# Attention, rational MLP and gated mixture on one core: the sign of 64-bit weights by parametric relu, early loads on ScalarE's queue, and extra matmuls behind attention's pieces

## The chip, the cores and the metric

The kernel runs on one core of a Trainium2 chip. The metric is the device time of one execution in microseconds; the engines are TensorE (PE, with its weight loads as PEld), VectorE (DVE), ScalarE (ACT), GpSimd (POOL) and SyncE (SP).

## The reference, cut to what is computed

Local attention over 4 batches of 8 heads, 576 positions of 64 values; four heads see the last 32 positions, four see every fourth of the last 128. Its output, as 2304 rows of 512, goes through a rational layer and then through eight experts with a gate that is balanced over rows and columns.

```python
x = attn_out.transpose(0, 2, 1, 3).reshape(B * S, H * D)
h = x @ w_in                                     # 512 -> 2048
P = a[0] + a[1]*h + a[2]*h**2 + a[3]*h**3
Q = 1.0 + abs(b[0])*abs(h) + abs(b[1])*h**2
x = (P / (Q + 1e-06)) @ w_out                    # 2048 -> 512
gate = balanced(exp(x @ w_gate - max))           # 8 rounds over rows and columns
out = sum(gate[:, e:e+1] * (relu(x @ w1[e]) @ w2[e]) for e in range(8))
```

`w_in` and `w_out` arrive as 64-bit floats; the kernel turns them into 32-bit floats itself.

## The kernel before

**Stages.** Batch 0 of attention runs first, by itself. Then 96 steps of the rational layer follow (`NS1`; six blocks of 384 rows, sixteen column blocks of 128), into whose slots, four to a step, the pieces of batches 1 (steps 0 to 7), 2 and 3, the conversion of weights and other side work are laid by hand with `at(slot, function)`. Then come the experts in 7-matmul units.

**Attention's pieces.** A batch is four pairs of heads with three groups of queries each. `att_pieces` gives 16 pieces `prep` (transposes of q or k into a PSUM bank, L347, evacuated by ACT, L355), 12 `qk` (mask matmul L363, scores L370; then DVE's maximum L388, ACT's exponentials L390, DVE's L394 and reciprocal L395, POOL's scaling L396), 12 `tr` (transposes of the weights, L405, evacuated at L410) and 12 `av` (L429; then a split into two 16-bit halves, ACT L229 and DVE L232). What a piece does after its matmuls is held back until the next piece has been laid down. In batch 0 the functions in `extra[i]` follow piece i (before: w_in's two first chunks asked for after pieces 12 and 30, w_gate's preparation after 20).

**The order of the work.** Each engine works off its own queue in order. The order on each queue is worked out by the framework from the order of the program, dependencies and priorities with estimated durations, so it is not always that of the text: conversions laid in later slots can stand earlier. `load` starts a transfer on SyncE's queue and makes it wait for the matmul last noted in `gate_mm`; in batch 0 that is the mask matmul of the last `qk` piece, later the first matmul of a step. Loads of v for attention (L302 to L315) wait on the same queue for their buffers.

**Conversion.** `to_f32` takes the high word of a 64-bit float as a 32-bit one, and ACT scales it by 2^-112 (L492); DVE shifts it left by 3, which drops the sign (L496), puts in three bits of the low word (L497), and the sign bit of the high word (L498). It runs on 16 pieces of w_in (four chunks `c` of four `kk`; `wi_conv`) and 16 rows of w_out (`wo_split`). ACT then takes each w_in piece's absolute maximum (L527), `wi_scale` makes a scale of it through a matmul (`across_max`, L180), and `wi_split` makes 16-bit halves, which the rational layer's matmuls (L631 to L633) read; its second layer is L691 to L693. The activation table is set once, at L239.

## Time and profile before

| | |
|---|---|
| median of 3 runs | 1973.75 us (1969.55 to 1974.08) |
| the profiled execution | 1978.19 us, its span 1976.1 us |
| PE busy | 1886.4 us, 95% of the span |
| DVE busy | 1567.5 us, 79% |
| ACT busy | 1217.0 us, 62% |
| POOL busy | 491.1 us, 25% |

Busy time is a sum of instructions' durations on an engine, without its waits; a matmul's end is modelled. The granted clock (PEclk) is 1.00 at 2.4 GHz and 0.50 at 1.2 GHz, and a value in between is a mean over a stretch. A row of the timeline gives the start, the duration, the instruction and, in brackets, how long its engine was idle before it and what ended that. `SPq` rows are the issue of transfers on SyncE's queue.

### The profile page before, as it was taken

What the parts mean: (1) busy time and instruction counts of PE and PEld (TensorE: products, weight loads), DVE (VectorE), ACT (ScalarE), POOL (GpSimd) and SP (SyncE); (2) the same over time, 40 slices, a digit from 0 to 9 for tenths busy, and PEclk for the clock granted to TensorE, in tenths of its full rate; (3) what the DMA queues carried; (4) which work ended last, traced back from release to release, by engine and by line L of the source; (5) the groups of instructions that cost most, each with busy time, mean ns of one, the idle gap of its engine ahead of it and who ended that gap; (6) DMA issues with size and microseconds to landing.
All of it is one profiled execution on the core that took longest, in us unless ns stands there. A gap on an engine that the chain in (4) does not pass through costs nothing. (4 is left out here: it accounts for less than half of the span.)

```text
span 1976.1 us, 36600 instructions
## 1 busy us (share of the span) xinstructions
PE 1886.4 (95%) x14202; PEld 1418.3 (72%) x14202; DVE 1567.5 (79%) x2564; ACT 1217.0 (62%) x2182; POOL 491.1 (25%) x489
## 2 busy tenths in 40 slices
PE   6688999998999999999999999999999999999998
PEld 5466777776767677767777777777777777777776
DVE  5797788799997998778787777877877787786754
ACT  5777777775776645646565664655555565555542
POOL 1232334321222113014212311411421141141111
PEclk7789999999999999999999999999999999999999
DMA  6643221124310451565356346345435625543323
GB/s 181 165 140 87 50 68 34 34 67 144 109 44 17 150 163 59 175 171 155 68 136 154 69 110 174 68 103 142 111 62 131 166 65 117 159 91 79 83 56 53
DMA packets 213133, 207.92 MB, mean 105 GB/s; under 512 B 78432, under 2 KB 160864, under 8 KB 212960
## 3 DMA queue, kind: packets, MB, share of 16 engines
q1 hardware_dynamic: 196096, 173.09, 29.1%
q0 software_dynamic: 16864, 32.51, 11.0%
q8 instruction: 111, 1.82, 0.4%
q14 instruction: 62, 0.51, 0.1%
HBM read 155.86 MB, written 49.68 MB: 104 GB/s over the span
## 5 line engine op out<-in xcount | busy, mean ns | idle before, releaser
L921 PEld LDWEIGHTS <-roomA 128*128 128x128 f16 x3276 | 319.7, 98 | 181.5 <-issue 14.6
L921 PE MATMUL l1a<-roomA 128*128 128x384 f16 x1872 | 357.0, 326 | 5.3 <-ACT roomV L970 4.2
L921 PE MATMUL l1b<-roomA 128*128 128x384 f16 x1404 | 273.6, 326 | 4.0 <-DVE roomA L972 1.9
L943 POOL TENSOR_TENSOR roomIG<-roomA 128x384 f32<-128x384 f32 x48 | 59.7, 1244 | 455.6 <-ACT roomA L977 354.6
L1021 PE MATMUL yps<-roomA 128*128 128x256 f16 x630 | 169.7, 273 | 2.2 <-DVE roomV L1047 1.5
L1022 PE MATMUL yps<-roomA 128*128 128x256 f16 x630 | 170.7, 273 | 0.8 <-DVE roomA L884 0.8
L1022 PE MATMUL yps<-roomA,roomV 128*128 128x256 f16 x630 | 170.5, 273 | 0.1
L677 POOL TENSOR_TENSOR roomIG<-roomA,roomIG 128x384 fp32r<-128x384 f32 x96 | 116.6, 1225 | 213.6 <-ACT roomIG L676 184.1
L1023 PE MATMUL yps<-roomA,roomV 128*128 128x256 f16 x630 | 169.6, 273 | 0.0
L1023 PE MATMUL yps<-roomA 128*128 128x256 f16 x630 | 168.9, 273 | 0.0
L1021 PE MATMUL yps<-roomA,roomV 128*128 128x256 f16 x630 | 168.8, 273 | 0.1
L692 PE MATMUL o1ps<-roomIG,roomV 128*128 128x384 f32 x384 | 136.2, 355 | 4.0 <-POOL roomIG L677 3.8
L870 POOL TENSOR_TENSOR roomA<-roomA 128x256 f32<-128x256 f32 x140 | 130.7, 953 | 35.2 <-DVE roomA L884 23.3
L631 PE MATMUL h1ps<-roomA 128*128 128x384 f16 x384 | 130.5, 340 | 8.8 <-ACT p L390 4.2
L884 DVE SCALAR_TENSOR_TENSOR roomA<-roomA,sm 128x768 f16<-128x768 f32 (+1 forms) x92 | 114.5, 1257 | 24.7 <-ACT roomA L881 23.9
L693 PE MATMUL o1ps<-roomIG,roomV 128*128 128x384 f32 x384 | 130.6, 340 | 0.0
L632 PE MATMUL h1ps<-roomA 128*128 128x384 f16 x384 | 130.1, 339 | 0.3 <-DVE roomA L232 0.3
L633 PE MATMUL h1ps<-roomA 128*128 128x384 f16 x384 | 129.8, 338 | 0.0
L943 POOL TENSOR_TENSOR roomIG<-roomV 128x384 f32<-128x384 f32 x48 | 50.1, 1044 | 299.5 <-ACT roomV L977 248.7
L691 PE MATMUL o1ps<-roomIG,roomV 128*128 128x384 f32 x384 | 107.5, 363 | 15.9 <-ACT roomIG L676 15.8
L1021 PEld LDWEIGHTS <-roomA 128*128 128x128 f16 x1008 | 98.7, 98 | 28.5 <-DVE roomA L1047 3.4
L881 ACT ACTIVATE roomA<-roomA,sm 128x768 f16<-128x768 f32 (+1 forms) x92 | 93.7, 1035 | 37.4 <-POOL roomA L870 17.8
(224 smaller groups left out, 4958.3 us busy)
## 6 DMA issues: line engine op xcount, KB each, us to landing
roomA<-xd SPq DMA_DIRECT2D x119, 384.0 KB
roomA<-in_moe_w_dram SPq DMA_DIRECT2D x256, 128.0 KB
roomA<-in_moe_w_dram SPq DMA_DIRECT2D x128, 256.0 KB
out_dram<-roomV POOLq DMA_DIRECT2D x31, 512.0 KB, 5.8
out_dram<-roomA POOLq DMA_DIRECT2D x31, 512.0 KB, 5.8
roomV<-in_moe_w_in_dram SPq DMA_DIRECT2D x16, 512.0 KB
roomA<-in_moe_w_out_dram SPq DMA_DIRECT2D x16, 512.0 KB
xd<-roomA SPq DMA_DIRECT2D x14, 384.0 KB
```

The lines of the kernel that those rows point to most:

```text
L631: mm = nc.tensor.matmul(hp, whi, xb[:, 0, kk, :], start=kk == 0, stop=False)
L632: nc.tensor.matmul(hp, whi, xb[:, 1, kk, :], start=False, stop=False)
L633: nc.tensor.matmul(hp, wlo, xb[:, 0, kk, :], start=False, stop=kk == KD - 1)
L677: nc.gpsimd.tensor_tensor(out=gl, in0=g, in1=gh.bitcast(F32), op=ALU.subtract)
L692: nc.tensor.matmul(ob[dd], hi, d["gl"], start=False, stop=False)
L693: nc.tensor.matmul(ob[dd], lo, d["gh"], start=False, stop=last)
L870: pin("p" if pool else "v", eng.tensor_tensor(out=d[:, o, :], in0=a, in1=b, op=ALU.add if w == 0 and n == 0 else ALU.subtract))
L884: pin("v", nc.vector.scalar_tensor_tensor(out=l, in0=x, scalar=sc, in1=h, op0=ALU.mult, op1=ALU.subtract))
L921: mm = nc.tensor.matmul(ps, w[:, wx_, wh, kk * P:(kk + 1) * P], x[:, xh, kk, :], start=start and kk == 0 and wh == 0 and xh == 0, stop=sto ...
L1021: nc.tensor.matmul(o, hh[:, a - 1, c], w[:, m, 0, :], start=i == 0 and half == 0, stop=False)
L1022: nc.tensor.matmul(o, hh[:, a - 1, c], w[:, m, 1, :], start=False, stop=False)
L1023: nc.tensor.matmul(o, hl[:, a - 1, c], w[:, m, 0, :], start=False, stop=i == NP - 1 and (last or half == 1 or b == 3))
```

## The change

The new `keep_busy` lays matmuls of 224 columns of the identity, read as 16-bit floats, behind the matmuls of a piece of batch 0 (four of them) or 1 (two), into columns of the same PSUM bank that the piece doesn't use; `prep`, `qk` and `av` pieces call it. In `to_f32` ACT applies a parametric relu with the slope -2^32 for negative values in place of a copy: a negative value becomes positive with an exponent higher by 32, whose bit DVE's shift moves to the sign. DVE's third operation goes. The first three loads of v for the maximum and those of w_in's chunks 0 and 1 move to ACT's queue, after pieces 4, 12 and 22; a `prep` piece of batch 0 now also notes its last matmul in `gate_mm`. Chunk 0 is converted after pieces 27 to 33 and split after 45 to 48, chunk 1 is converted after 37 to 46 and split in slots 2 to 8. w_gate is loaded at step 20 and prepared at step 26.

```diff
--- before.py
+++ after.py
@@ -20,7 +20,6 @@
 NEG = -1.0e9
 EXP_MASK = 0x7F800000
 ABS_MASK = 0x7FFFFFFF
-SIGN = -(1 << 31)
 TINY = 2.0**-80
 LN_SHIFT = 63
 
@@ -162,8 +161,8 @@
 
     gate_mm = [None]
 
-    def load(out, in_):
-        i = nc.sync.dma_start(out=out, in_=in_)
+    def load(out, in_, eng=nc.sync):
+        i = eng.dma_start(out=out, in_=in_)
         if gate_mm[0] is not None:
             tc.add_manual_dep(i.ins, gate_mm[0].name, mybir.DependencyInfo(mybir.DependencyClass.Sync, mybir.DependencyReason.DATA), reason="paced load")
 
@@ -240,6 +239,13 @@
     ident = cpool.tile([P, P], F32, name="ident")
     make_identity(nc, ident)
     nc.vector.memset(one, 1.0)
+    ident_w = ident.bitcast(BF16)
+
+    def keep_busy(bt, b, c, count):
+        if b < 2:
+            for _ in range(count):
+                nc.tensor.matmul(bt[:, c:c + 224], ident_w[:, 0:P], ident_w[:, 0:224], start=True, stop=True)
+
     ident_b = cpool.tile([D, P], BF16, name="ident_b")
     nc.vector.tensor_copy(ident_b.rearrange("p (h c) -> p h c", h=2), ident[0:D, 0:D].unsqueeze(1).to_broadcast([D, 2, D]))
     SEAMS = (0, None, None, None, 32, None, 0, None, 16, 48, -16, None)
@@ -344,7 +350,10 @@
         w, n = (QB, 3) if pr < 2 else (72, 4)
         bt = bank("qkps")
         for c in range(n):
-            nc.tensor.transpose(bt[:, c * w:(c + 1) * w], src[:, n * y + c, :], ident[:w, :w])
+            mm = nc.tensor.transpose(bt[:, c * w:(c + 1) * w], src[:, n * y + c, :], ident[:w, :w])
+        keep_busy(bt, b, HS, 4 - 2 * b)
+        if b == 0:
+            gate_mm[0] = mm.ins
 
         def after():
             if pr < 2:
@@ -374,6 +383,7 @@
                     start=False,
                     stop=i == 2,
                 )
+        keep_busy(bt, b, 3 * KW, 4 - 2 * b)
         sc = bt[:, 0:3 * KW].rearrange("q (i c) -> q i c", i=3)
         i = b * NG + pr * 3 + jj
         sx = sb.tile([P, 4, 3], F32, tag="asx", bufs=4, name="sx")
@@ -433,6 +443,8 @@
                     start=True,
                     stop=True,
                 )
+
+        keep_busy(bt, b, 288, 4 - 2 * b)
 
         def after():
             pos, end = GQ * jj, GQ * (jj + 1)
@@ -475,7 +487,7 @@
 
     def v_load(hf, i, tag):
         t = vst[hf, i] = stage_home(tag, "vst")
-        load(out=t, in_=vflat[hf, :, i * NV:(i + 1) * NV])
+        load(out=t, in_=vflat[hf, :, i * NV:(i + 1) * NV], eng=nc.sync if hf else nc.scalar)
 
     def v_scan(hf, i):
         t = vst.pop((hf, i))
@@ -489,13 +501,12 @@
     def to_f32(src, y, dst):
         w = src.rearrange("p (n two) -> p n two", two=2)
         lo, hi = w[:, :, 0], w[:, :, 1]
-        nc.scalar.activation(y, hi.bitcast(F32), AF.Copy, scale=float(2.0**-112))
+        nc.scalar.activation(y, hi.bitcast(F32), AF.Prelu, scale=float(2.0**-112), alpha=-float(2.0**32))
         d = y.bitcast(I32)
 
         def bits():
             nc.vector.tensor_scalar(out=d, in0=d, scalar1=3, scalar2=None, op0=ALU.logical_shift_left)
-            nc.vector.scalar_tensor_tensor(out=d, in0=lo, scalar=29, in1=d, op0=ALU.logical_shift_right, op1=ALU.bitwise_or)
-            nc.vector.scalar_tensor_tensor(out=dst.bitcast(I32), in0=hi, scalar=SIGN, in1=d, op0=ALU.bitwise_and, op1=ALU.bitwise_or)
+            nc.vector.scalar_tensor_tensor(out=dst.bitcast(I32), in0=lo, scalar=29, in1=d, op0=ALU.logical_shift_right, op1=ALU.bitwise_or)
 
         return bits
 
@@ -515,7 +526,7 @@
                 if kk % 2 == 0:
                     t = room(WI_ST[c][kk // 2], [P, 2, 1024], I32)
                 wst[c, kk] = t[:, kk % 2, :]
-                load(out=wst[c, kk], in_=src)
+                load(out=wst[c, kk], in_=src, eng=nc.scalar if c < 2 else nc.sync)
             else:
                 nc.sync.dma_start(out=wx[c][:, kk, :], in_=src)
 
@@ -570,7 +581,7 @@
     wi = [None] * 4
 
     def wi_scale(c):
-        return pow2_scale(wmx[:, 4 * c:4 * c + 4], 4, 14, s_wi[:, c:c + 1], i_wi[:, c:c + 1], lag=3 if c > 1 else 0, then=lambda: coefs(0, c, c + 1))
+        return pow2_scale(wmx[:, 4 * c:4 * c + 4], 4, 14, s_wi[:, c:c + 1], i_wi[:, c:c + 1], lag=3, then=lambda: coefs(0, c, c + 1))
 
     def wi_split(c, kk):
         if kk == 0:
@@ -584,8 +595,7 @@
     def wg_prep():
         m = cols()
         nc.vector.tensor_reduce(out=m, in_=wgr.rearrange("p k e -> p (k e)"), axis=AX, op=ALU.max, apply_absolute_value=True)
-        pow2_scale(m, 1, 4, s_wg, i_wg)
-        split16(wgr, wg[:, :, 0:NE], wg[:, :, NE:], s_wg)()
+        return pow2_scale(m, 1, 4, s_wg, i_wg, lag=3, then=lambda: split16(wgr, wg[:, :, 0:NE], wg[:, :, NE:], s_wg)())
 
     wo_hi, wo_lo = [], []
 
@@ -1136,7 +1146,7 @@
     LAG = 5
     ATT = ((1, 0, 7), (2, 7, 23), (3, 40, 62))
     WO = [f + f // 7 if f < 8 else 20 + 2 * (f - 8) for f in range(NF1)]
-    WI_S = (None, 0, 8, 14)
+    WI_S = (None, None, 8, 14)
 
     def att_pieces(b):
         groups = [(pr, jj) for pr in range(H // 2) for jj in range(3)]
@@ -1284,14 +1294,18 @@
             if callable(more):
                 at(s + 1, more)
 
-    for c in range(1, 4):
+    for kk in range(KD):
+        at(2 + 2 * kk, wi_split, 1, kk)
+    for c in range(2, 4):
         s = 4 * WI_S[c]
         for kk in range(KD):
             at(s + 1 + 2 * kk, wi_conv, c, kk)
-            at(s + (14 if c > 1 else 11) + kk, wi_split, c, kk)
+            at(s + 14 + kk, wi_split, c, kk)
         at(s + 10, wi_scale, c)
     for c in (2, 3):
         at(4 * WI_S[c] - (16 if c == 2 else 14), wi_load, c)
+    at(4 * 20, lambda: load(wgr, w_gate.rearrange("(k p) e -> p k e", p=P)))
+    at(4 * 26 + 1, wg_prep)
     for i in range(3):
         at(4 * 1 + 8 * i, v_load, 1, i, "x2_4")
         at(4 * (1 + 2) + 8 * i, v_scan, 1, i)
@@ -1305,27 +1319,26 @@
     att_load(0, 1, "R1")
     nc.sync.dma_start(out=abt[:, 0:4], in_=ra.partition_broadcast(P))
     nc.sync.dma_start(out=abt[:, 4:6], in_=rb.partition_broadcast(P))
-    for i in range(3):
-        v_load(0, i, f"x2_{3 + i}")
     att_load(0, 2, "R2")
     for i in range(2, 4):
         att_load_v(i)
     for i in range(4, 8):
         att_load_v(i)
-    nc.sync.dma_start(out=wgr, in_=w_gate.rearrange("(k p) e -> p k e", p=P))
     att_load(0, 3, "R3")
     pcs = att_pieces(0)
     extra = defaultdict(list)
+    extra[4].append(lambda: [v_load(0, i, f"x2_{3 + i}") for i in range(3)])
     extra[12].append(lambda: wi_load(0))
-    extra[30].append(lambda: wi_load(1))
+    extra[22].append(lambda: wi_load(1))
     av0 = next(i for i, pc in enumerate(pcs) if pc[0] == "av")
     extra[av0 - 1] += [lambda i=i: v_scan(0, i) for i in range(3)] + [lambda: v_scale(0), coef0]
-    extra[20] += [wg_prep]
     n = len(pcs)
     for kk in range(KD):
-        extra[30 + 2 * kk].append(lambda kk=kk: wi_conv(0, kk))
-        extra[n - 4 + kk].append(lambda kk=kk: wi_split(0, kk))
-    extra[n - 4 - 1].append(lambda: wi_scale(0))
+        extra[27 + 2 * kk].append(lambda kk=kk: wi_conv(0, kk))
+        extra[45 + kk].append(lambda kk=kk: wi_split(0, kk))
+        extra[37 + 3 * kk].append(lambda kk=kk: wi_conv(1, kk))
+    extra[40].append(lambda: wi_scale(0))
+    extra[50].append(lambda: wi_scale(1))
     for f in range(2):
         extra[44 + f].append(lambda f=f: wo_load(f))
     later = []
```

## Rows read from the trace of the kernel before

**Rows 1.** Busy time by stretch: us, then each engine's us (count), clock, DMA share.
```profile
0.00:68.90 68.90, 45.71 (x398) 35.52 (x398) 37.51 (x121) 38.92 (x146) 11.43 (x33) 0.69 0.73 196
...
4.40:20.00 15.60, 11.97 (x117) 9.69 (x117) 6.95 (x21) 6.78 (x30) 2.00 (x3) 0.89 0.77 232
20.00:36.00 16.00, 12.95 (x100) 9.82 (x99) 7.89 (x33) 7.67 (x33) 2.81 (x5) 0.60 0.57 121
36.00:52.80 16.80, 12.47 (x113) 9.57 (x111) 10.11 (x25) 11.83 (x45) 2.91 (x4) 0.57 0.60 177
...
58.70:68.90 10.20, 8.33 (x71) 6.41 (x71) 10.16 (x36) 10.20 (x36) 1.21 (x3) 0.50 1.13 269
...
68.90:150.00 81.10, 67.47 (x529) 48.74 (x529) 69.72 (x148) 62.17 (x189) 26.85 (x29) 0.84 0.43 130
150.00:200.00 50.00, 41.83 (x314) 29.62 (x313) 38.44 (x92) 37.41 (x103) 10.99 (x12) 0.93 0.32 86
200.00:320.00 120.00, 117.05 (x815) 88.19 (x812) 101.30 (x173) 93.52 (x208) 45.37 (x42) 0.99 0.22 58
...
470.00:500.00 30.00, 21.19 (x107) 16.93 (x106) 29.97 (x52) 14.49 (x24) 5.60 (x5) 0.83 0.26 77
...
1000.00:1800.00 800.00, 793.03 (x6063) 592.80 (x6062) 633.36 (x932) 463.18 (x667) 206.09 (x201) 1.00 0.47 113
```

**Rows 2.** Timeline, 68 to 72 us: start, us, instruction; first L631, later matmuls.
```profile
68.93 0.50 PE L631 MATMUL h1ps<-roomA 128*128 128x384 f16 x1
...
71.31 0.33 PE L632 MATMUL h1ps<-roomA 128*128 128x384 f16 x1
...
71.47 0.33 PE L633 MATMUL h1ps<-roomA 128*128 128x384 f16 x1
```

**Rows 3.** Waits until 68.9 us: who waited for whom, us, times, longest.
```profile
PE qkps L347 <- DMA roomA<-in_q_dram: 5.1, 2, 4.4
...
DVE sm L586 <- DMA wgr<-in_moe_w_gate_dram: 3.6, 1, 3.6
```

**Rows 4.** Timeline, 45 to 59 us: start, us, instruction, idle before it.
```profile
45.46 7.31 SPq L315 DMA_DIRECT2D roomA<-in_v_dram  x13
...
52.82 1.87 SPq L166 DMA_DIRECT2D roomV<-in_moe_w_in_dram  x4
...
57.17 0.66 ACT L492 ACTIVATE roomV<-roomV 128x512 f32<-128x512 f32 x1 [5.95 <-DMA roomV<-in_moe_w_in_dram]
...
58.76 0.85 PE L405 MATMUL ptps<-ident,roomA 128*96 128x128 f32 x3 [6.08 <-DVE roomA L232]
```

**Rows 5.** Timeline, 31 to 41 us.
```profile
31.48 0.79 PE L180 MATMUL mxps<-ident,sm 128*128 128x128 f32 x2 [1.02 <-DVE sm L586]
...
38.72 0.66 ACT L492 ACTIVATE roomV<-roomV 128x512 f32<-128x512 f32 x1 [4.30 <-DMA roomV<-in_moe_w_in_dram]
...
40.77 1.17 PE L429 MATMUL avps<-roomA 96*64 96x64 f32 x12 [2.09 <-ACT roomA L410]
```

**Rows 6.** Busy time in three finer stretches of batch 0.
```profile
24.00:30.00 6.00, 6.00 (x50) 4.42 (x49) 1.12 (x5) 3.03 (x12) 0.63 (x1) 0.50 0.38 85
46.00:50.00 4.00, 4.00 (x42) 3.41 (x44) 3.53 (x9) 3.56 (x14) 0.00 (x0) 0.50 0.49 109
50.00:52.70 2.70, 2.68 (x33) 2.00 (x30) 0.56 (x4) 1.22 (x8) 1.33 (x2) 0.91 0.22 49
```

**Rows 7.** Lines 498, 527, 166: min/median/max ns (L527: busy us, mean ns).
```profile
L498 DVE SCALAR_TENSOR_TENSOR roomA<-roomA x16: 660/684/1481, 74.3 to 316.6; 128x512 int32<-128x512 int32 x16
...
L527 ACT ACTIVATE roomV<-roomV 128x512 f32<-128x512 f32 x8 | 5.1, 634 | 0.0
...
L166 SPq DMA_DIRECT2D roomV<-in_moe_w_in_dram x16: 423/430/653, 33.3 to 177.2; - x16
```

**Rows 8.** Waits of PE, 68.9 to 200 us.
```profile
PE qkps L347 <- DVE roomA L657: 2.9, 2, 1.5
```

**Rows 9.** ACT's only table load: busy us, mean ns, idle before.
```profile
L239 ACT ACT_TABLE_LOAD x1 | 1.3, 1283 | 0.8 <-PEq L1405 0.8
```

## Prediction

> **What bounds the kernel now.** I read the table of stages first [rows 1]. From 1000 to 1800 us TensorE (PE) is busy 793 of 800 us and runs at its full clock, and between 200 and 320 us already 117 of 120; the one large hole in between is 470 to 500 us (21.2 of 30 us busy), where VectorE (DVE) is at 29.97 of 30. What comes after 200 us is therefore a stream of matmuls of fixed length, and a microsecond saved before it is a microsecond off the end, unless a new hole opens. The loss sits in front: until 68.9 us, where the first matmul of the rational layer (L631) starts [rows 2], PE is busy 45.7 us, and from there to 200 us 109 of 131 us, with clocks of 0.69, 0.84 and 0.93.
>
> The second view is who waited for whom before 68.9 us [rows 3]: PE 5.1 us for q, DVE 3.6 us for w_gate; and ScalarE (ACT) over 10 us for chunks of w_in, which the next view places. The timeline shows the largest of these [rows 4]: SyncE's queue spends 45.5 to 52.8 us on thirteen small loads of v, and only then issues the second chunk of w_in; ACT, first in, first out, stands at that chunk's conversion until 57.17 us, and PE starts nothing until 58.76 us, after 6.1 idle. The same pattern is smaller at 33 to 39 us and, for w_gate, at 28 to 32 us [rows 5].
>
> The third view is the granted clock in fine windows [rows 6]: 0.50 all through 24 to 30 us although PE counts as busy; up in the 51st us after four dense microseconds; and after the idle stretch of 52.7 to 58.7 us it is down to 0.50 for all of 58.7 to 68.9 us [rows 1].
>
> **The change part by part.** The sum is made on the profiled execution, 1978.2 us with a span of 1976.1, which lies 4.4 us over the median of 1973.75 us; differences are then taken off the median.
>
> *Batch 0, loads.* (a) The second chunk of w_in is asked for after piece 22 instead of 30, on ACT's queue, where no load of v stands before it. Landing took 4.35 us from issue [rows 4], so it is there some 20 us before its conversion. The hole of 52.8 to 58.7 us goes: -5.9. (b) The first chunk likewise after piece 12. ACT stood idle 4.3 us for it, PE 2.1 us after that [rows 5]: -2.1 to -4.3, taken as -3. (c) w_gate's preparation leaves batch 0 for step 26. DVE idled 3.6 us for it, PE 1.0 us [rows 3, 5]: -1.0 to -3.6, taken as -2.5, as the reciprocal of the softmax stood behind it on DVE. At step 26 its handful of operations of 0.1 to 0.3 us finds its data long landed: 0 to +1, taken as +0.5. What DVE waits for the coefficients stays: that load keeps its place on SyncE's queue.
>
> (d) The price is ACT's time. Eleven loads (three of v, eight of w_in) move to ACT's queue; SyncE took 0.43 us to issue one [rows 7], so 4.7 us of ACT, plus what each waits for the matmul that paces it; the exponentials and evacuations of attention are queued behind, and PE's next transposes wait for these. ACT is busy 38.9 of 68.9 us: 0 to +4.7, taken as +2. All transfers but the 16 KB of w_gate are the same bytes. At 46 to 52.7 us the DMA engines were busy 22 to 49% [rows 6] while the second chunk was missing, so what was late was the issue, behind SyncE's loads of v, and (a) and (b) count in full. The Trainium skill speaks against this part (DMA: Bandwidth & Descriptors, Issuing engines are not separate DMA queues): DMAs of all issuing engines run on the same 16 DMA engines, and several issuers save only issue time. By that alone (a) and (b) would give nothing, and the sum would be 9 us poorer; with a queue that waits for buffers, as here, the trace does not agree.
>
> *Sign by parametric relu.* (e) The third DVE operation of each conversion (L498) goes, 32 times 0.68 us [rows 7], 21.9 us of DVE in all, eight of them (5.4 us) in batch 0. There DVE was full (10.16 of 10.2 us) only from 58.7 us on [rows 1], where half of the eight stand: 0 to -5.4, taken as -2. ACT's operation is assumed as long as the copy it replaces, 0.66 us [rows 5]; the trace has no parametric relu, so I bound it by ACT's other operation over the same 512 columns, the absolute maximum (L527), 0.63 us [rows 7], and by it again with half as much on top: -0.03 to +0.3 us each, up to 10 us of ACT over 300 us in which it is busy some three quarters [rows 1]; taken as nothing.
>
> *Extra matmuls.* (f) Batch 0 has 40 pieces of the three kinds, so 160 extra matmuls of 224 bf16 columns, batch 1 has 80. A 384-column matmul starts every 0.16 us at full clock [rows 2], which is 0.32 at half, so an extra costs 0.095 or 0.187 us: 15.2 or 29.9 us in batch 0, 7.6 or 15 us in batch 1. They stand behind their piece on PE, and in the piece's own bank, so I let the evacuation wait for them: 0.38 or 0.75 us a piece in batch 0. What they can buy: by the clocks of [rows 1], 32 of the 45.7 us of PE before 68.9 us ran at half (80% of 20 to 36 us, 86% of 36 to 52.8, all of 58.7 to 68.9, 22% of 4.4 to 20). All at full clock, PE's work is 29.7 us, with the extras 44.9: as much as before. The gain is that nothing else slows down with it; I take 0, with bounds of -8 (half of the 16 us saved lies on the chain and the extras fill holes) and +20 (below).
>
> Batch 0 so far: -5.9 -3 -2.5 +2 -2 +0 = -11.4. L631 would start near 57.5 us.
>
> *Batch 1 and after.* (g) Twenty-four more L498 go, 16.4 us of DVE between 69 and 317 us. PE waited there for DVE's L657 2.9 us between 68.9 and 200 us [rows 8] and was idle 3.0 us between 200 and 320 [rows 1]: 0 to -6, taken as -4. (h) Clock: by the means of [rows 1] 26 us of 68.9 to 150 us and 7 us of the next 50 ran at half, worth some 14 us. These follow holes in which PE waits for ACT or DVE, and an extra stands behind the piece that waits, so it fills no hole; it only makes the rest denser. A quarter: -3 (0 to -8). (i) The 80 extras of batch 1 stand in a stage where PE is busy 83%: 0 to +15, taken as +4, about half of 7.6 us. (j) w_in's second chunk is split in steps 0 to 2 rather than 2 to 3: ACT and DVE work of the same size, 0.
>
> Batch 1 and after with w_gate: -4 -3 +4 +0.5 = -2.5. Together **-14**, so 1973.75 - 14 = **1960 us**.
>
> **The rivals.** *A, PE becomes the bound in batch 0 (slower).* If the extras don't bring the clock up, PE's 45.7 us stay, the extras cost 70% of 0.187 and 30% of 0.095 us, 25.5 us in all, and PE alone needs 4.4 + 71.2 = 75.6 us, 6.7 past 68.9, whatever the loads gain; batch 1 adds 5 or so of its 7.6 to 15 us. That gives 1985 us. It decides from a mean clock in batch 0 of about 0.7 downward. For it: 24 to 30 us, busy throughout and still at 0.50. Against it: the rise after 46 to 50 us, where PE ran without pauses, and that the idle stretch that sent the clock down at 57 us is gone.
>
> *B, the gain is hidden (no change).* ACT, with 4.7 us more to do and stopped by each load that waits for its pacing matmul, takes the place of the stalls, and the big chunks, now sent while the DMA engines carry v and the third pair's q and k at 77% [rows 1], make PE wait longer for small loads (5.1 us for q already, 4.4 of them in one wait [rows 3]). Terms (a) to (c) halve to -5.7, (d) goes to +4.7, the rest stays without the clock: -5.7 +4.7 -2 -4 +4 +0.5 = -2.5, 1971 us.
>
> *C, the change does not do what it says.* The trace has one table load on ACT, 1.28 us at the start [rows 9]. Were parametric relu in another table than the exponential, most of 32 conversions would be put between two more loads, up to 82 us of ACT; with half on the path, 2015 us. Against it: the copy, abs, exp and ln that share ACT now never cause a second load. The Trainium skill (ScalarE: Activation LUTs, Table sets: the hidden batching unit) says that cheap functions are in every set but does not name this one, and prices a switch at about 2.66 us, by which 64 switches would be an estimated 170 us; no row here has a second switch.
>
> **How the numbers follow.** Forecast 0.70, A 0.14, B 0.13, C 0.03. The forecast's own ends: with every unknown at its good bound some -35 us, at its bad bounds short of A about -3. 1940 to 1978 leaves out most of A, all of C, and the outermost tenth of the forecast. About 0.3%, 6 us, is what a measurement of this kernel tells from no change. The forecast is faster by more than that in nine of ten of its cases (0.63), B in a quarter of its own (0.03): 0.66. Within it lie the forecast's last tenth and most of B: 0.17. Slower: A and C, 0.17.
>
> **What would show it.** Right: L631 starts at 55 to 60 us; no wait of ACT for w_in before it; the clock of 20 to 50 us over 0.8; L498 of the old form gone with ACT's conversion at 0.66 to 0.68 us; still a single table load; from 320 us on the same picture, shifted. Wrong: a clock of 0.5 with PE busy without holes in batch 0 (A); ACT waiting for PE at the loads it now issues, or PE for q and k (B); table loads between conversions (C); or a hole of other length at 470 to 500 us, where DVE sets the pace and nothing is changed, which would move the end by several us for a reason not in the sum.

## The result, and the profile after

The changed kernel takes **1986.85 us** (median of 7 runs, 1982.56 to 1995.22) where the kernel before takes 1974.08: ratio 1.007 [1.0056, 1.0084]. It is slower by some 12.8 us; the forecast was 1960. Two stray executions of the experiments (7981 us of e5, 6214 us of the kernel before beside e9) are in a slow state and left out of the medians below. In the profiled execution (span 1983.3 us) the first matmul of the rational layer starts at 74.0 us, before at 68.9 [rows 2]; the forecast said 57.5.

The stages of the changed kernel, columns as in [rows 1] (stretch, then each engine's busy us, clock, DMA share):

```profile
0.00:68.90 68.90, 48.33 (x489) 37.86 (x489) 31.75 (x100) 38.12 (x139) 10.55 (x31) 0.88 0.73 196
68.90:150.00 81.10, 74.46 (x605) 51.56 (x606) 51.28 (x125) 56.56 (x178) 22.01 (x27) 0.87 0.40 123
150.00:200.00 50.00, 44.84 (x368) 33.72 (x366) 40.37 (x101) 43.01 (x117) 11.94 (x15) 0.97 0.34 96
200.00:320.00 120.00, 115.80 (x820) 88.03 (x819) 99.74 (x176) 95.62 (x212) 45.54 (x42) 1.00 0.22 58
470.00:500.00 30.00, 26.33 (x141) 20.74 (x140) 30.00 (x40) 16.14 (x26) 8.12 (x6) 0.94 0.42 122
1000.00:1800.00 800.00, 793.80 (x6064) 592.84 (x6063) 635.05 (x937) 463.68 (x669) 206.79 (x201) 1.00 0.48 115
...
500.00:520.00 20.00, 16.39 (x95) 11.49 (x94) 19.71 (x44) 12.59 (x21) 6.38 (x4) 0.91 0.27 91
```

The clock of the first 68.9 us rose from 0.69 to 0.88, as the extra matmuls were meant to do (without them, in e2 below, it is 0.66 again). The experts' row is the same. The hole of 470 to 500 us is spread out: PE is idle 3.7 us there and 3.6 us in the next 20, together 7.3 us from 470 to 520 where the kernel before has 9.0, with DVE at 30.00 of 30 and 19.71 of 20. From the start of step 64 to that of step 72, the steps around it, both kernels take the same time (43.1 us before, 42.9 after).

What took the place of the old stalls in batch 0 is in ScalarE's timeline (start, us, instruction, in brackets the idle time before it and what ended it; ACTq is ACT issuing a load):

```profile
22.36 2.01 ACTq L165 DMA_DIRECT2D roomV<-in_moe_w_in_dram  x4
24.41 0.49 ACT L420 ACTIVATE roomA<-ptps 96x384 f32<-96x384 f32 x1 [7.48 <-DMA roomA<-in_v_dram]
...
33.46 8.67 ACTq L165 DMA_DIRECT2D roomV<-in_moe_w_in_dram  x4
42.18 0.34 ACT L400 ACTIVATE p<-scps,sx 128x96 f32<-128x96 f32 x1 [9.54 <-DMA roomV<-in_moe_w_in_dram]
```

ACT stands 7.5 and 9.5 us **at its own loads of w_in**, with evacuations and exponentials queued behind. The loads of both queues tell of their landing by eight semaphores, taken in turn over SyncE and ACT together, and a load waits until the one eight earlier has landed. In the trace ACT stands from 16.9 to 22.3 us for a load of k that SyncE had issued at 10.7, and its next three loads wait until 23.8, the last of them for a load of v; the longest part of the second stretch, 36.3 to 41.8 us, is for a load of q that SyncE had issued at 34.2. Why that load of k took over 11 us to land no run shows. Who pays is in the waits until 80 us (who waited for whom, us, times, longest):

```profile
PE avps L439 <- ACT roomA L420: 14.9, 4, 7.5
ACT p L400 <- DMA roomV<-in_moe_w_in_dram: 9.5, 1, 9.5
ACT roomA L364 <- PE qkps L247: 7.8, 7, 3.9
ACT roomA L420 <- DMA roomA<-in_v_dram: 7.5, 1, 7.5
```

The third line is attention's evacuation waiting for the extra matmuls (L247) in its bank; before, the same evacuation waited 3.3 us for its own transposes until 69 us.

The loss is not simply carried from the front to the end. The changed kernel is 13.9 us behind at the start of step 4 and only 1.9 us at that of step 36 (310.2 against 308.3); the last conversion by parametric relu starts at 305.7 us, w_gate is split by 285.5 and the last extra starts at 156.6, so nothing of the edit comes later. Yet the last matmul of the rational layer's first layer starts 11.8 us behind (617.7 against 605.9). Against the trace of e9, whose order is that of before (see below), the two lags are 5.4 and 14.0 us: the growth is the same to 1.3 us.

Parametric relu did what it says: still one table load, and the conversion (L504) takes ACT as long as the copy did [rows 5]:

```profile
L504 ACT ACTIVATE roomV<-roomV x16: 642/672/682, 31.4 to 190.7; 128x512 f32<-128x512 f32 x16
```

### The profile page after: what moved, and what is told of

It reads as the page before. It is cut to its first block, busy times and chain, and to the rows that moved or that the text cites. A ratio compares the mean times of both kernels' runs of the same rounds, so it can differ in the third digit from the quotient of the medians.

```text
span 1983.3 us, 37051 instructions
## 1 busy us (share of the span) xinstructions
PE 1903.1 (96%) x14442; PEld 1430.2 (72%) x14442; DVE 1550.6 (78%) x2532; ACT 1217.8 (61%) x2182; POOL 493.6 (25%) x489
## 5 line engine op out<-in xcount | busy, mean ns | idle before, releaser
L641 PE MATMUL h1ps<-roomA 128*128 128x384 f16 x384 | 128.8, 336 | 3.8 <-DVE roomA L231 3.4
L894 DVE SCALAR_TENSOR_TENSOR roomA<-roomA,sm 128x768 f16<-128x768 f32 (+1 forms) x92 | 112.6, 1237 | 22.3 <-ACT roomA L891 21.3
L642 PE MATMUL h1ps<-roomA 128*128 128x384 f16 x384 | 128.3, 334 | 0.0
L643 PE MATMUL h1ps<-roomA 128*128 128x384 f16 x384 | 128.0, 333 | 0.0
L1031 PEld LDWEIGHTS <-roomA 128*128 128x128 f16 x1008 | 98.7, 98 | 28.4 <-DVE roomA L1057 3.4
L1032 PEld LDWEIGHTS <-roomV 128*128 128x128 f16 x1008 | 98.7, 98 | 25.1 <-issue 1.9
```

The source lines that it names most:

```text
L641: mm = nc.tensor.matmul(hp, whi, xb[:, 0, kk, :], start=kk == 0, stop=False)
L642: nc.tensor.matmul(hp, whi, xb[:, 1, kk, :], start=False, stop=False)
L643: nc.tensor.matmul(hp, wlo, xb[:, 0, kk, :], start=False, stop=kk == KD - 1)
L894: pin("v", nc.vector.scalar_tensor_tensor(out=l, in0=x, scalar=sc, in1=h, op0=ALU.mult, op1=ALU.subtract))
L1031: nc.tensor.matmul(o, hh[:, a - 1, c], w[:, m, 0, :], start=i == 0 and half == 0, stop=False)
L1032: nc.tensor.matmul(o, hh[:, a - 1, c], w[:, m, 1, :], start=False, stop=False)
```

## The experiments

Theory 1: ACT standing for its own loads makes the loss. Theory 2: the extra matmuls make it. Theory 3: the new places of conversions and w_gate. Theory 4 came after the first four runs: the framework orders every engine's queue anew by estimated durations, and that order decides. The kernel before ran beside each group, at 1974.6, 1972.8, 1973.5, 1973.4 and 1974.1 us; the changed kernel ran in the first measurement alone. "First" and "last" are the starts of the first and last matmul of the rational layer's first layer; before has 68.9 and 605.9. Both come from one trace of each run, and so do all starts of steps below. The traces of before and of e9, in which PE and ACT work in the same order, differ by 1 to 4 us from step 0 to the last, so a lead or lag of that size in one trace says nothing.

| run | kernel | first | last | median us | ratio to before |
|---|---|---|---|---|---|
| e1 | after, loads on SyncE | 72.4 | 603.5 | 1975.2 | 1.0004 [0.9992, 1.0017] |
| e2 | after, no extras | 69.1 | 606.6 | 1976.3 | 1.0010 [1.0001, 1.0020] |
| e3 | before + extras | 67.9 | 612.1 | 1979.9 | 1.0032 [1.0021, 1.0043] |
| e4 | before + relu | 66.0 | 609.9 | 1978.4 | 1.0022 [1.0008, 1.0036] |
| e5 | before + spare op, 3rd | 69.1 | 617.3 | 1982.9 | 1.0049 [1.0034, 1.0064] |
| e6 | before + spare op, 10th | 69.0 | 613.5 | 1979.6 | 1.0037 [1.0019, 1.0054] |
| e7 | after + spare op, 10th | 75.7 | 618.1 | 1981.6 | 1.0042 [1.0027, 1.0056] |
| e8 | after, SyncE, no extras | 71.2 | 610.5 | 1976.7 | 1.0016 [1.0002, 1.0030] |
| e9 | before + spare op, 24th | 67.7 | 603.7 | 1974.3 | 1.0004 [0.9990, 1.0019] |
| e10 | after, loads on GpSimd | 67.3 | 607.5 | 1973.7 | 1.0007 [0.9990, 1.0023] |
| e11 | before, no durations | 60.8 | 606.0 | 2030.7 | 1.0296 [1.0278, 1.0314] |
| e12 | after, no durations | 74.7 | 589.8 | 2009.2 | 1.0189 [1.0167, 1.0211] |
| e13 | after, order laid down | 75.2 | 590.8 | 1957.75 | 0.9920 [0.9901, 0.9939] |
| e14 | before, order laid down | 60.9 | 606.4 | 1971.6 | 0.9986 [0.9973, 0.9998] |
| e15 | before + relu, order held | 67.7 | 604.5 | 1970.9 | 0.9985 [0.9971, 0.9998] |
| e16 | before + extras, order held | 72.5 | 609.5 | 1975.6 | 1.0013 [0.9999, 1.0028] |
| e17 | e13 without extras | 73.8 | 584.0 | 1951.2 | 0.9890 [0.9863, 0.9917] |
| e18 | e13 with the copy | 82.0 | 604.0 | 1972.9 | 0.9990 [0.9980, 1.0001] |

**e1 to e4, parts one by one** (edits shortened, here and below).

```
e1, on after:   eng=nc.scalar if c < 2 else nc.sync   ->  eng=nc.sync    (and v likewise)
e2, on after:   keep_busy: if b < 2                   ->  if b < 0
e3, on before:  + keep_busy and its three calls
e4, on before:  AF.Copy -> AF.Prelu, alpha=-2**32; third DVE operation removed
```

> The changed kernel with the early loads of v and w_in back on SyncE's queue; their places in the program, the extra matmuls and the parametric relu stay. Theory 1 (ACT stands for its own loads: it is idle 7.5 and 9.5 us in front of them, since a load waits for an earlier transfer of any queue): both holes of ACT go, the first matmul of the rational layer comes 8 to 17 us earlier than in the changed kernel (57 to 66 instead of 74.0 us), the time is 1967 to 1977 us. Theory 2 (the extra matmuls lengthen batch 0): the first matmul of the rational layer stays at 70 to 74 us and the time within 4 us of the changed kernel, 1983 to 1991 us. Theory 3 (the order of the conversions and w_gate, laid elsewhere, costs the time): as theory 2.

> The changed kernel without its extra matmuls. Theory 1: the two holes of ACT stay, the time falls by 0 to 5 us, to 1982 to 1987 us. Theory 2: PE has 15 to 25 us less to do in batch 0 and 8 in batch 1, evacuations wait for less, and the time falls by 10 to 20 us, to 1967 to 1977 us. Theory 3: within 4 us of the changed kernel. The granted clock of 0 to 75 us tells what the extras bought: 0.69 without them if they set it, about 0.87 if something else does.

> The kernel before with the extra matmuls alone. Theory 2: 8 to 20 us slower than the kernel before, 1982 to 1994 us. Theory 1: within 5 us of the kernel before, the first matmul of the rational layer at 66 to 72 us, with the clock of batch 0 over 0.8 if the extras set it.

> The kernel before with the parametric relu in place of the third VectorE operation, nothing else. By the prediction's term it is worth 2 us in batch 0 and 4 behind it: 1968 us. If VectorE's time is hidden before 320 us, within 3 us of the kernel before. One table load at the start, the new operation at 0.66 to 0.68 us; if it were a second table, over 2000 us.

Taking either part away from the changed kernel gives back nearly all of the loss (11.7 us for the queue, 10.6 for the extras), so they do not add up. e1's time is the one of theory 1, but the first matmul comes at 72.4 us and not at 57 to 66, and ACT now waits 12.3 us for w_in at its conversions. e2's time is the one of theory 2, with ACT's holes still there (10.4 and 7.3 us) and the first matmul at 69.1 all the same. e3 fits neither theory's time (1982 or more; within 5 us of before). And relu alone, which only takes DVE work away and starts the rational layer 2.9 us sooner, came out 3.8 us slower, outside both of its expectations. No theory of parts explains that. In e4 the lead was 10.7 us at step 7 and was gone at the last step.

**e5, e6, e9: the order alone.** The order on the queues shows why: in the traces, PE's sequence of matmuls in e4 leaves that of before at 50.6 us. So I put in one operation on one column, which changes no result, at different conversions:

```
+ if n == 3 (e5), 10 (e6), 24 (e9):  vector.scalar_tensor_tensor(out=d[:, 0:1], in0=lo[:, 0:1], scalar=29,
+     in1=d[:, 0:1], op0=logical_shift_right, op1=bitwise_or)
```

> The kernel before with one spare operation of one column (under 0.1 us of VectorE, its result the same) put into the third conversion of w_in. In the built program PE's order is as before up to the 214th matmul, in batch 0, and is another one from there until the 8752 matmuls of the experts, which stand as before. Theory 4 (the framework orders each engine's queue anew by estimated durations, and where DVE sets the pace between 430 and 620 us the new order decides what is left of a gain or a loss): the time differs from 1974.6 by 3 to 8 us, either way, and the end of the rational layer from 631 us by as much, though the work is the same. Theories 1 and 2 (only the waits of ACT and the extra matmuls count): within 2 us of 1974.6.

> The same spare operation of one column in the tenth conversion: batch 0's order is untouched, PE's differs from the 398th matmul on, after the rational layer has begun. Theory 4: the first matmul of the rational layer stays at 68.9 us to within 1 us, yet the end moves by 3 to 8 us, either way, and not as in the run with the third conversion. Theories 1 and 2: within 2 us of 1974.6.

> The kernel before with the same spare one-column operation, now in the twenty-fourth conversion (a row of w_out): in the built program PE's and ACT's orders are exactly those of before, DVE's differs by the operation itself and a few neighbours. Theory 4 (the order, not the operation, cost the 11 and 7 us of the two earlier spare operations): within 3 us of before, 1970 to 1978, and the rational layer's end at 631 us to within 2. If the operation itself were the cost: 1979 to 1986 again.

First-layer matmuls of e5, e6 and e9 (count, least, median and most ns, first and last start):

```profile
L631 PE MATMUL h1ps<-roomA x384: 322/326/527, 69.1 to 617.3; 128*128 128x384 f16 x192
```
```profile
L631 PE MATMUL h1ps<-roomA x384: 322/326/528, 69.0 to 613.5; 128*128 128x384 f16 x192
```
```profile
L631 PE MATMUL h1ps<-roomA x384: 323/326/543, 67.7 to 603.7; 128*128 128x384 f16 x192
```

All three start within about 1 us of before, and the matmuls are as long. PE's sequence leaves that of before at 60.2 us in e5 and at 101.7 in e6; there the layer's last matmul starts 11.4 and 7.6 us later, and the time follows (+10.1, +6.8 us; e5's is beyond the 3 to 8 us expected). In e9 PE's and ACT's sequences are those of before, and nothing happens (+0.9 us, within the noise). e5 loses it late: 1.5 us behind at step 40, 8.6 at the last. Theory 4 holds. The operation was longer than the expected 0.1 us or less, 0.15 us in e5, 0.20 in e6 and 0.64 in e9, and the one that took longest cost nothing that shows.

**e7, e8, e10: the changed kernel again.**

```
e7:   after + the spare operation of e6
e8:   e1 and e2 together
e10:  eng=nc.gpsimd in place of nc.scalar for the eleven loads
```

> The changed kernel with the same spare operation in its tenth conversion: batch 0 stands as in the changed kernel, PE's order differs from the 460th matmul on. ACT's two holes (7.5 and 9.5 us, for its own loads) and the 160 extra matmuls of batch 0 are all there. Theory 1 with 2 (the loss is made in front, 5 to 14 us by step 4): 1987 within 2 us. Theory 4 (a good part of the 12 us is the order of the steps behind): first matmul of the rational layer at 74 us again, but a time 4 us or more away from 1987, either way.

> The changed kernel with all loads back on SyncE's queue and without the extra matmuls: what is left is parametric relu, w_in's chunks asked for after pieces 12 and 22, w_gate at step 26 and the new places of conversions and splits. Theories 1 and 2 as a sum: taking the queue away gave -11.7, taking the extras away -10.5, so both together about 1965 (1962 to 1970), and the first matmul of the rational layer near 64 us. Theory 4: the two do not add up; the first matmul comes 0 to 5 us earlier than 68.9, but of that lead less than half is left at the end of the rational layer, 1970 to 1979.

> The changed kernel with the eleven early loads on GpSimd's queue in place of ScalarE's; nothing else of the edit differs (the framework orders anew). In the built program these loads wait for the matmul that paces them and, the last three, for earlier loads of this queue, no longer for SyncE's loads. Theory 1 (ACT standing in front of its own loads made the holes): ACT's waits of 7.5 and 9.5 us and PE's 14.9 us for ACT are gone, the first matmul of the rational layer at 58 to 66 us (74.0 in the changed kernel). Rival: the holes come from the transfers themselves (too early, colliding with q, k and v), then ACT still waits 10 us or more for w_in and the first matmul stays at 70 to 75. Theory 4 says of the end that a lead of 8 us in front leaves anything from 1966 to 1982; theory 1 alone 1963 to 1968.

e7, with ACT's holes and extras all there, is 1981.6, some 5 us nearer to before than the changed kernel; its interval and the changed kernel's just touch, so this one is weak by itself. e8 isn't the 1965 that a sum of parts gives, and its rational layer even starts later (71.2): its conversion of w_in stood on ACT's queue 15.7 us ahead of its data. e10 settles the place in front: with the loads on POOL's queue no wait of ACT for a load is left, and the first matmul comes at 67.3 instead of 74.0 us. That lies between the two expectations, 58 to 66 and 70 to 75. The time is 13 us under the changed kernel's (1973.7), twice the lead in front; that the rest came with the new order follows from theory 4 and was not tested by itself.

**e11, e12: no estimated durations.**

```
- TileContext(nc, schedule_with_timeline_sim=True)
+ TileContext(nc, schedule_with_timeline_sim=False)
```

> The kernel before in the order of its own text: the framework's reordering by estimated durations is switched off, so no edit elsewhere moves an instruction. Meant as the partner of the next run. Slower than before, between 1985 and 2150, as conversions and attention pieces no longer move ahead of the steps they are written in.

> The changed kernel in the order of its own text. Against the run before it this is the change without any reordering. Theories 1 and 2: the same loss as with reordering, 8 to 16 us over the partner, and ACT again standing 5 us or more at its own loads. Theory 4: most of the 12 us was the order, so here the change is worth between -14 and +6 us.

The order is then made from the text, dependencies and priorities (pieces of attention still stand ahead of their text, so "the order of its text" says too much). Both are slower, by their experts, but the change is now worth **-21.5 us**, beyond the -14 of theory 4, and the last matmul of the rational layer's first layer starts 16 us sooner with it.

**e13, e14: the order laid down.** The first part's order of e12 and of e11 is written into the kernels as edges; the experts are ordered by durations again.

```
+ ORDER = {"EngineType.PE": "0-2 ...", ...}      # positions, per engine, until the last step
+ for i, j in zip(seq, seq[1:]):
+     tc.add_manual_dep(j, i.name, DependencyInfo(NoSync, DATA), reason="order")
```

> The changed kernel, with every engine's order up to the end of the rational layer's steps written down as it stood in its run without estimated durations (edges of order only, no semaphore), and the experts ordered by estimated durations as ever. Theory 4 (the order, not the edit, made the kernel slower): the rational layer ends 14 to 19 us before that of the kernel before, as in that run, and all of it reaches the end, since the experts are PE's: 1955 to 1962. Rival (the experts lose it again, by their loads or their order): 1970 or more.

> The partner: the kernel before with its own order without estimated durations up to the end of the rational layer, the experts ordered as ever. Its rational layer ended 0.5 us before that of before in that run: 1971 to 1977, the same as before. The difference to the run with the changed kernel is what the edit is worth in an order of the same making: 12 to 18 us. Rival (the laid order alone is the gain): this one is 10 us or more faster as well.

The same instructions as the changed kernel's, in another order: 1957.75 instead of 1986.85 us. Against the partner, which has edges of the same making and is 1.8 us faster than before, the change is worth **-13.9 us**. Start of the first matmul of a step, in us, from the timelines:

| step | before | after | e14 before laid | e13 after laid | e17 no extras | e18 copy |
|---|---|---|---|---|---|---|
| 0 | 68.9 | 74.0 | 60.9 | 75.2 | 73.8 | 82.0 |
| 4 | 112.3 | 126.2 | 117.7 | 117.7 | 109.2 | 122.5 |
| 16 | 214.3 | 218.3 | 216.4 | 204.2 | 196.1 | 212.2 |
| 40 | 324.9 | 328.2 | 337.8 | 322.1 | 313.5 | 334.0 |
| 64 | 459.8 | 467.0 | 467.8 | 450.8 | 442.2 | 464.1 |
| 72 | 502.9 | 509.9 | 501.8 | 484.8 | 476.2 | 498.1 |

After and e13 begin the rational layer alike; 8.5 us part them by step 4, 14 by step 16, 25 by step 72. The two laid kernels differ elsewhere: e13 begins 14.3 us later than e14, is level at step 4 and gains nearly 15 us from step 8 to 12, where e14 takes 43.2 us, e13 28.4 and before 30.8. There e14's PE waits for halves of w_out's rows:

```profile
PE o1ps L691 <- ACT roomV L609: 9.3, 2, 5.4
```

So the -13.9 us are in part a stall of the partner's own order, and not the edit's work alone. Against before in its own order e13 is 15.7 us faster. The stretch of 470 to 500 us of e13, where before and after have their hole:

```profile
470.00:500.00 30.00, 27.71 (x162) 22.50 (x161) 30.00 (x53) 20.42 (x32) 9.42 (x8) 1.00 0.31 95
```

DVE is as full as before (30.00), yet PE has 27.7 us of work instead of 21.2 [rows 1]. But e13 is at later steps by then. The same steps, 64 to 72, of before and then of e13:

```profile
459.80:502.90 43.10, 34.29 (x186) 25.95 (x185) 42.33 (x69) 23.16 (x36) 6.76 (x6) 0.88 0.33 98
```
```profile
450.80:484.80 34.00, 33.29 (x198) 26.14 (x198) 34.00 (x55) 21.69 (x37) 10.55 (x8) 1.00 0.29 89
```

DVE is full in both, but in before 69 of its operations (42.3 us) fall between these starts and in e13 55 (34.0 us): the order puts more of DVE's work into these steps, and PE waits for it. e14 takes 34.0 us for them too.

**e15, e16: one part each in the order of before.**

```
e15:  e4 with the order of before as edges, the third operations missing from it
e16:  e3 with the order of before as edges, each extra behind its piece
```

> The kernel before with parametric relu, every instruction of every engine up to the end of the rational layer in exactly the order of before, the 32 third operations of the conversions (21.9 us of DVE) simply missing. Free to be ordered anew, this change gave 1978.4 (+3.8). Theory 4: in the held order nothing is late, the lead that free ordering showed at steps 7 to 36 (5 to 10 us) stays: 1964 to 1970. Rival (DVE, full between 430 and 620 us, or the hole at 470 to 500 us, takes the lead whatever the order): 1972 to 1976.

> The kernel before with the 240 extra matmuls, each behind its piece on PE, and otherwise exactly the order of before. Free to be ordered anew, this change gave 1979.9 (+5.3). Theory 4: the extra matmuls themselves are worth little, the clock of batch 0 rises and the first matmul of the rational layer stays at 66 to 70 us: 1972 to 1977. Theory 2 (they lengthen batches 0 and 1 by themselves): 1979 to 1983.

Held, relu is worth -2.5 us (free: +3.8), the extras +2.2 (free: +5.3, interval when held -0.2 to +5.5). Both signs are now those of their work, though that of the extras is hardly clear of noise. 1970.9 lies between relu's two expectations: its lead over before was 4.9 us at step 40 and 1.3 at the last step. Whether full DVE takes back the rest, one trace can't tell: e9, which has all of DVE's work, leads before by 3.4 and 2.2 us at the same places. With the extras the first matmul came at 72.5 us, later than the 66 to 70 expected.

**e17, e18: what makes the 13.9 us.**

```
e17:  e13, keep_busy's matmuls taken out of code and order
e18:  e13, AF.Copy again, the third DVE operation directly behind the second
```

> The changed kernel in the laid order of the run that gave 1957.75, the 240 extra matmuls simply missing, no other instruction in another place. If the extra matmuls carry the gain by the clock (1.00 at 60 to 75 us with them, 0.50 in the partner without): the clock falls to 0.5 to 0.7 between 30 and 75 us, and the time rises by 4 to 10 us, 1962 to 1968. If they cost what they cost in the order of before (2.2 us): 1954 to 1957, and the moves carry the gain. Between: the two about cancel, within 2 us of 1957.75.

> The changed kernel in the laid order, with ScalarE's scaled copy in place of parametric relu and VectorE's third operation back, directly behind the second, 32 times 0.68 us. If VectorE's 21.9 us carry the gain: 1966 to 1972, and the loss grows in steps 8 to 40, where VectorE is busy 49.4 of 75 and 106.8 of 120 us. If they are worth what they were in the order of before (2.5 us): 1959 to 1963, and the moves carry the gain.

Stretches of e13, then of e17, then of e18:

```profile
30.00:60.00 30.00, 21.64 (x240) 17.15 (x238) 11.97 (x36) 19.77 (x70) 4.20 (x7) 0.89 0.72 181
60.00:75.00 15.00, 12.21 (x154) 9.86 (x153) 12.32 (x45) 14.35 (x51) 2.39 (x5) 1.00 0.55 153
...
200.00:320.00 120.00, 115.89 (x787) 89.58 (x786) 106.75 (x181) 100.00 (x214) 52.92 (x42) 0.99 0.19 52
```
```profile
30.00:60.00 30.00, 22.15 (x176) 16.79 (x175) 13.28 (x39) 20.02 (x74) 4.19 (x7) 0.58 0.72 178
60.00:75.00 15.00, 13.04 (x122) 10.60 (x122) 11.81 (x45) 14.00 (x50) 2.39 (x5) 0.61 0.59 160
```
```profile
30.00:60.00 30.00, 18.73 (x192) 15.06 (x191) 12.96 (x32) 15.72 (x59) 3.59 (x6) 0.77 0.71 182
...
200.00:320.00 120.00, 112.67 (x779) 87.04 (x779) 112.87 (x196) 96.76 (x213) 50.64 (x42) 0.99 0.20 55
```

Without the extras the clock of 30 to 75 us falls back to 0.6, and the kernel is 6.5 us **faster**, below every expectation: the first matmul comes at 73.8 instead of 75.2 us, and by step 4 the lead is 8.5. With the copy it is 15.1 us slower (0.9 over the range expected if DVE's time carries the gain): 6.9 of them are there at step 0, 12 at step 40, and PE is busy 112.7 instead of 115.9 us of the 120 in which DVE has 6 us more. So in this order relu carries -15.1 and the extras +6.5. The rest, -13.9 + 15.1 - 6.5 = -5.3 us if the three add up, is the moved loads and conversions together with all else in which the two laid orders differ, the partner's stall included; no run parts these. e17, at 1951.2 us, is faster than both kernels: 23 us under before.

## Why the prediction was wrong

**The step that failed** is the premise of the sum: that what comes after 200 us is a stream of fixed length, so that a microsecond saved in front is one off the end. It took every duration, wait and hole from one order of the queues and kept that order. The text itself said that the order is worked out by the framework; no term, bound or rival had a price for a new one. The runs give that price: +6.8 and +10.1 us for a spare operation of 0.20 and 0.15 us, and 29 us between two orders of the changed kernel.

The sum for the front failed as well: it had the first matmul of the rational layer at 57.5 us, and no run made from the changed kernel has it before 67.3 (e10). With the order laid down in the same way for both, the change came to -13.9, and the sum had said -14. That is luck: there the changed kernel begins the rational layer 14.3 us later than its partner, where the sum had 11.4 us earlier, and the gain comes nearly all from steps 0 to 12.

The ends of the forecast were summed wrongly too. By the bounds of its own terms the good end is some -41 us and not -35. The bad one is +4 and not -3 with (i) at the 7.6 us of a full clock, and +12, or 1985 us, with (i) at its 15.

*(a) to (d), loads and ACT's time.* That ACT no longer stands at the conversions (5.95 and 4.30 us before [rows 4, 5]) was right; the wait went to the loads themselves, 7.48 and 9.54 us. (d) had +2 us, at most 4.7, for issuing eleven loads "plus what each waits for the matmul that paces it"; the wait that came was for other loads, and 17.0 us long. [rows 4] was read rightly: SyncE's 7.31 us for thirteen small loads are mostly issue, 0.3 to 0.7 us each. What the rows did not tell, and no term had, is that a load also waits for the landing of an earlier one, whichever of the two queues that one stands on. The rule of the Trainium skill that the prediction set aside (DMA: Bandwidth & Descriptors, Issuing engines are not separate DMA queues: another issuer saves only issue time) fits these runs better than the prediction did: on SyncE's queue and on GpSimd's (e1, e10) the kernel takes 1975.2 and 1973.7 us, each in an order of its own. That ACT's queue costs 11.7 and 13.1 us more the rule does not say. With the order laid, the moves and whatever else the two orders differ in are worth -5.3 us, where (a) to (d) with the 0.5 of w_gate summed to -8.9.

*(e) and (g), relu.* Taken at -2 and -4 us, bounded by -5.4 and -6. In the order of before it gave -2.5, in the laid order -15.1, beyond both bounds together. The operation's length was right (0.67 us for the copy's 0.66). Mis-sized was how much of DVE's work lies on the path, which a row of busy time does not tell and another order changes.

*(f), (h), (i), the extras.* The rise of the clock was right (0.58 to 0.89 in 30 to 60 us of e17 and e13). (f) at 0 was nearly right for batch 0 in the laid order (1.4 us between e13 and e17); in the order of before the extras put the first matmul 3.6 us later (e16), and taking them out of the changed kernel put it 4.9 us earlier (e2). (h), -3 us for the clock, did not come in the laid order: from 75 to 150 us the clock is 0.91 with the extras and 0.93 without. (i) at +4, about half of its 7.6 us, came there at nearly the full price: 7.1 us from step 0 to step 4, in which e13's PE is busy 41.4 of 42.5 us. Held in the order of before all the extras together cost 2.2.

*The rivals.* A gave 1985 us, close to the result, by a clock that stays low; the clock rose, so the number met and the mechanism did not. B named what happened in front, ACT stopped by its loads, but priced it with 2.7 us more than the forecast and for another reason. C is out: one table load. Of the signs of a wrong prediction, one came in part: ACT stands at the loads it issues, though for other loads and not for PE. The other, a hole of another length at 470 to 500 us, came by the clock on the wall only; by steps it is as long as before and explains none of the 12.8 us. That the end moves "for a reason not in the sum" came true all the same, and should have been a rival with a chance.

**What stays open.** I did not try other orders of the laid kind, so nothing says that 1951 us is the best one, or how much of the 13.9 us another pair of orders would show; the orders of before's own work that ran gave 1971.6 to 1982.9 us with the experts ordered by durations. Which instruction's new place makes the changed kernel lose some 9 us behind step 36, where nothing of the edit stands any more, was not followed to its end. Nor was the split of the 12.8 us between ACT's holes and the later order measured by a run of its own: e13, which starts the rational layer as late as the changed kernel, says that the late start alone need not cost anything.

## What to carry to other kernels

Where a framework orders the queues by estimated durations, compare the built orders before believing a difference of one per cent, and hold the order (edges without semaphores) when one edit is to be priced: here one and the same edit is +12.8 or -13.9 us. Hold it for both kernels, and look in the partner too for a stall that only its order has. A load issued from a computing engine's queue stops that engine for whatever the load waits for, other loads too; put it where nothing is queued behind it. Extra matmuls can raise TensorE's clock and still be pure cost: ask whether PE sets the pace there before buying clock, and what the extras cost where it does.

## What was not expected of the hardware

A higher clock, bought with extra matmuls, did not shorten its stretch: what lies ahead of the rational layer ran, from 30 us on, at 0.89 to 1.00 with the extras and at 0.58 to 0.61 without, and it ended at 75.2 and 73.8 us. PE was busy 34.0 us of it in both, so that the clock paid for the extras and for nothing else. And a load issued on ACT's queue can stop ACT until an earlier load of SyncE's queue has landed, here 5.4 us for one of k and 5.5 us for one of q.
